# Attention, mixture of experts and FFN on one core: the third batch's loads of k and q move behind a store of x

## The chip, the core and the metric

The kernel runs on one core of a Trainium2 chip. The metric is device time in microseconds (us), and lower is better. The core has five instruction streams that matter here. TensorE (PE in the profile, PEld for its weight loads) multiplies and transposes. VectorE (DVE) and ScalarE (ACT) do element work. GpSimd (POOL) does small additions. SyncE (SP) computes nothing: in this kernel it asks for nearly all the direct transfers between memory and the core. Each stream runs its instructions in the order in which the program gives them.

## The reference

Three parts follow one another: block-causal attention over 4 batches of 8 heads (576 positions, head size 64), then a mixture of 8 experts with one expert for each token, then a dense FFN.

```python
scores = scale * np.matmul(q, k.transpose(0, 1, 3, 2))        # q, k, v: (4, 8, 576, 64)
scores = np.where(block_i >= block_j, scores, -1000000000.0)  # blocks of 64
attn = np.exp(scores - scores.max(-1, keepdims=True))
attn = attn / (attn.sum(-1, keepdims=True) + 1e-09)
x = np.matmul(attn, v).transpose(0, 2, 1, 3).reshape(2304, 512)
# expert e for the tokens whose gate is largest at e
out[mask] = gate_w[mask, None] * (np.maximum(xe @ w1[e], 0.0) @ w2[e])
# dense FFN
h = x @ w_in
g = np.maximum(h, 0.0) + np.log1p(np.exp(-np.abs(h)))
return g @ w_out
```

## The kernel before

Only the attention at the start (the first 240 us or so) matters for this change. It works on 16 **pairs** of heads, numbered 0 to 15. A batch has four pairs, so the first batch is pairs 0 to 3, the second 4 to 7 and the third 8 to 11. For a pair p the program transposes k and q (Kta.p, Qta.p, Ktb.p, Qtb.p, line 332), multiplies the scores (S0.p, S1.p, S2.p, line 378), takes maxima on DVE (line 384) and exponentials on ACT (line 389), transposes the probabilities (T, line 395), multiplies them with v (V.p, line 410), turns the result back into rows of x (Xa.p, Xb.p on PE, line 425) and scales these rows by the softmax's sums (xa.p, xb.p on DVE, lines 443 and 444). The scaled rows go into the tile xs, and xo.p stores them to the scratch tensor xd with two transfers asked for on SP (lines 450 and 451). Pairs overlap: while S0.p, S1.p and S2.p run, V.(p-1) follows and the rows of pair p-2 are made. What stands from one S0.p to the next is called **stage p** below.

The order of all this is written out by hand in one long string, SCHEDULE. Each word of it is one step, and the steps are issued in that order, each to its engine. Two buffers tie the steps together:

- xs exists once (line 436), so xa.p may not write it before both transfers of xo.(p-1) have landed.
- The tag ps2, a bank pair of PSUM, also exists once. The accumulators that xa.p and xb.p read (psx, line 421) and the widest scores of S0.(p+2) and S1.(p+2) (s4, line 356) share it. So S1.(p+2) may not start its part s4 before xb.p has read psx.

The loads of a batch b are the steps b1.0 to b1.17, b2.0 to b2.17 and so on (line 291): six transfers of k (four of 256 KB, two of 128 KB), then six of q, then six of v. They fill one of two buffers for each of k, q and v, so the third batch's k and q take the buffers of the first batch and wait on PE until Ktb.3 and Qtb.3 have read those. The first batch is loaded in slices of heads (f0 to f47, line 280). At the start of the kernel all these loads stand in one line on SP. The transfers asked for on SP use eight completion semaphores in turn (DMAHW0 to DMAHW7): a transfer waits on SP until the one eight places ahead of it has landed, and a step that needs a transfer's end waits for its semaphore.

```python
    XS[p][1] = work.tile([128, 5, 2, D], F32, tag="xs", name="xs", bufs=1)       # line 436, in x_out
    nc.sync.dma_start(xv[0:64], xs[0:64, 0]...)                                  # line 450, in x_st
    nc.sync.dma_start(xv[64:].rearrange("(c p) e -> p c e", p=128), xs[:, 1:5]...)
```

Of the kernel before, what the change touches and what calls it, by code (L numbers as in the profile page):

```python
# [20 lines left out]
NT, DM, E, F1, F2 = 2304, 512, 8, 1024, 2048  # L21
# [36 lines left out]
h21.0 h01.0 Klb.2 m30.1 S2.1 m41.1 e30.1 m20.1 T11.0 e41.1 m00.1 T30.0 m10.1 e00.1 m21.1 h11.0 m11.1 e20.1 h30.0 V.0  # L58
e10.1 e21.1 e11.1 Xr.1 F1.0 S0.2 F0.0 m40.2 T10.1 T20.1 m31.2 h10.1 Kta.3 e40.2 h20.1 T00.1 Qta.3 m01.2 Kha.3 T31.1
h00.1 Kla.3 Xa.0 Qha.3 h31.1 e31.2 Xb.0 Qla.3 T21.1 e01.2 xa.0 T01.1 xb.0 xo.0 b1.10 b1.11 f42 f43 f44 f45 f46 f47  # L60
b1.12 b1.13 b1.14 b1.15 b1.16 b1.17 Ktb.3 Qtb.3 h01.1 h21.1 S1.2 b2.0 La.0 b2.1 b2.2 b2.3 Qhb.3 b2.4 b2.5 Khb.3 b2.6
b2.7 Qlb.3 b2.8 b2.9 Klb.3 b2.10 b2.11 m30.2 S2.2 m41.2 e30.2 m20.2 T11.1 e41.2 m00.2 T30.1 m10.2 e00.2 m21.2 h11.1
m11.2 e20.2 h30.1 V.1 e10.2 e21.2 e11.2 Xr.2 F1.1 S0.3 F0.1 m40.3 T10.2 T20.2 m31.3 h10.2 Kta.4 e40.3 h20.2 T00.2 Qta.4
m01.3 Kha.4 T31.2 h00.2 Kla.4 Xa.1 Qha.4 h31.2 e31.3 Xb.1 Qla.4 T21.2 e01.3 xa.1 T01.2 xb.1 xo.1 Ktb.4 Qtb.4 h01.2
h21.2 S1.3 La.1 et Qhb.4 Khb.4 Qlb.4 Klb.4 m30.3 S2.3 m41.3 e30.3 m20.3 T11.2 e41.3 m00.3 T30.2 m10.3 e00.3 m21.3 h11.2
m11.3 e20.3 h30.2 V.2 e10.3 e21.3 e11.3 Xr.3 F1.2 S0.4 F0.2 m40.4 T10.3 T20.3 m31.4 h10.3 Kta.5 e40.4 h20.3 T00.3 Qta.5
m01.4 Kha.5 T31.3 h00.3 Kla.5 Xa.2 Qha.5 h31.3 e31.4 Xb.2 Qla.5 T21.3 e01.4 xa.2 T01.3 xb.2 xo.2 Ktb.5 Qtb.5 h01.3
h21.3 S1.4 La.2 Qhb.5 Khb.5 Qlb.5 Klb.5 m30.4 S2.4 m41.4 e30.4 m20.4 T11.3 e41.4 m00.4 T30.3 m10.4 e00.4 m21.4 h11.3
# [1523 lines left out]
```

## Time and profile before

| | |
|---|---|
| median of three runs | 903.48 us (903.44 to 903.62) |
| the profiled execution | 902.99 us |
| its span, first to last instruction | 901.3 us |
| PE busy | 876.0 us (97%) |
| DVE busy | 663.8 us (74%) |
| ACT busy | 562.9 us (62%) |
| mean granted TensorE clock | 0.995 of full speed |

The profiled execution took 902.99 us, 1.69 us more than its span, and the median of the runs is 0.49 us above it. All times inside the kernel are counted from the start of the span. A stretch of idle time of PE counts as time of the kernel where nothing else could have run; idle time of the other engines counts only where PE waits for them.

### The profile page before, as it was taken

The page shows a single profiled execution, that of the slowest core. Times are in us where ns is not written, and L with a number is a line of the kernel's source. Part 1 is how long each engine was busy: PE and PEld are TensorE (multiplying, and loading weights), DVE is VectorE, ACT ScalarE, POOL GpSimd, SP SyncE. Part 2 cuts the span into 40 slices and gives each one's busy share as a digit, 9 for nine tenths or more (in the row PEclk, how much of TensorE's full clock was granted, in tenths as well). Part 3 has the DMA queues.
Part 4 walks back from the last instruction along what each step waited for, and adds up shares of the span by engine and source line. Part 5 has one row for each costly group of instructions (what it writes and reads, how often), then busy time and mean ns, then how long its engine had stood idle before and what let it go on. Part 6 is the DMA issues. An engine that isn't in the chain of part 4 may idle for free.

```text
span 901.3 us, 17961 instructions
## 1 busy us (share of the span) xinstructions
PE 876.0 (97%) x6165; PEld 768.5 (85%) x6165; DVE 663.8 (74%) x1502; ACT 562.9 (62%) x1252; POOL 131.6 (15%) x165
## 2 busy tenths in 40 slices
PE   8979999999999999999999999999999999999997
PEld 5867887787899889999898887888788999999997
DVE  5656768968699898865764567676676569888975
ACT  5655676668556577655855688787778734343332
POOL 1010000010112252222310100000000001541421
PEclk9998999999999999999999999999999999999999
DMA  5894722433424468976361566466665883434323
GB/s 117 184 196 86 144 54 55 159 85 121 143 83 135 151 204 281 316 246 219 116 215 59 161 220 202 164 203 220 229 247 198 247 305 116 153 116 143 129 71 106
DMA packets 138486, 148.63 MB, mean 165 GB/s; under 512 B 70800, under 2 KB 95888, under 8 KB 138385
## 3 DMA queue, kind: packets, MB, share of 16 engines
q1 hardware_dynamic: 132240, 132.37, 48.5%
q0 software_dynamic: 4800, 14.70, 4.8%
q8 instruction: 50, 0.82, 0.4%
q10 hardware_dynamic: 1344, 0.33, 0.2%
q14 instruction: 52, 0.42, 0.2%
HBM read 119.56 MB, written 41.43 MB: 179 GB/s over the span
## 4 chain that ended last, share of the span: by engine, by line
PE 56%; DVE 4%; DMA 3%; issue 1%; ACT 1%; SPq 1%; DVEq 0%; ACTq 0%
PE yps L1062 3%; PE yps L1063 3%; PE yps L1064 3%; PE fh L1206 3%; PE fh L1207 3%; PE fh L1205 3%; PE hps L1027 3%; PE hps L1028 3%; PE hps L1029 3%; DMA gq<-gd 2%; PE fX L1206 2%; PE fX L1207 2%; PE fX L1205 2%; PE fY L1206 2%; PE fY L1207 2%; PE fY L1205 2%
## 5 line engine op out<-in xcount | busy, mean ns | idle before, releaser
L1335 ACT CAST ah<-sum 128x1280 fp32r<-128x1280 f32 (+1 forms) x40 | 46.3, 1157 | 107.6 <-DVE sum L1328 40.5
L389 ACT ACTIVATE P<-s,negm 128x448 f32<-128x448 f32 (+4 forms) x160 | 82.7, 528 | 32.8 <-DVE negm L384 32.8
L1027 PE MATMUL hps<-xh,H1h 128*128 128x256 f32 x320 | 90.8, 284 | 0.2 <-DVE hl L1047 0.2
L1029 PE MATMUL hps<-xh,H1l 128*128 128x256 f32 x320 | 90.5, 283 | 0.0
L1028 PE MATMUL hps<-xl,H1h 128*128 128x256 f32 x320 | 90.5, 283 | 0.0
L384 DVE TENSOR_REDUCE negm<-s 128x1 f32<-128x576 f32 (+4 forms) x160 | 68.3, 479 | 19.1 <-PE s L378 19.0
L983 DVE TENSOR_TENSOR H2l<-R,H2h 128x512 fp32r<-128x512 f32 x96 | 63.6, 687 | 25.4 <-ACT H2h L979 22.2
L1400 POOL DMA_INDIRECT out_dram<-fos,OI x16 | 47.2, 2952 | 198.8 <-DVE fos L1392 154.8
L979 ACT CAST H2h<-R 128x512 fp32r<-128x512 f32 x96 | 57.5, 624 | 27.2 <-PE yps L1063 11.9
L395 PE MATMUL pt<-ident,P 128*128 128x128 f32 x480 | 68.8, 280 | 3.0 <-DVE PT L400 2.0
L1062 PE MATMUL yps<-H2h,hh 128*128 128x512 f32 x176 | 71.6, 407 | 0.2 <-PEq L1532 0.2
L378 PE MATMUL s<-kZ,qZ 64*128 64x288 f32 (+4 forms) x576 | 62.0, 328 | 9.9 <-DVE lg L444 7.1
L1063 PE MATMUL yps<-H2h,hl 128*128 128x512 f32 x176 | 68.8, 391 | 0.0
L1064 PE MATMUL yps<-H2l,hh 128*128 128x512 f32 x176 | 68.7, 390 | 0.0
L983 DVE TENSOR_TENSOR H1l<-R,H1h 128x512 fp32r<-128x512 f32 x96 | 62.3, 685 | 8.3 <-ACT H1h L979 6.3
L378 PEld LDWEIGHTS s<-kZ,qZ 64*128 64x128 f32 x576 | 52.6, 193 | 18.4 <-issue 13.4
L979 ACT CAST H1h<-R 128x512 fp32r<-128x512 f32 x96 | 55.5, 622 | 16.2 <-PE hps L1028 11.5
L1339 DVE TENSOR_TENSOR al<-sum,ah 128x1280 fp32r<-128x1280 f32 (+1 forms) x40 | 54.2, 1356 | 13.5 <-ACT ah L1335 13.5
L1027 PEld LDWEIGHTS hps<-xh,H1h 128*128 128x128 f32 x320 | 61.3, 192 | 0.8 <-DVE hl L1047 0.4
L1028 PEld LDWEIGHTS hps<-xl,H1h 128*128 128x128 f32 x320 | 61.3, 192 | 0.3
L1029 PEld LDWEIGHTS hps<-xh,H1l 128*128 128x128 f32 x320 | 61.3, 192 | 0.0
L395 PEld LDWEIGHTS pt<-ident,P 128*128 128x128 f32 x480 | 53.1, 142 | 7.0 <-DVE PT L400 2.7
(361 smaller groups left out, 2623.6 us busy)
## 6 DMA issues: line engine op xcount, KB each, us to landing
R<-in_moe_w_dram SPq DMA_DIRECT2D x96, 512.0 KB
gd<-ft SPq DMA_DIRECT2D x64, 256.0 KB
gq<-gd SPq DMA_DIRECT2D x64, 256.0 KB
dbw<-in_moe_w_out_dram SPq DMA_DIRECT2D x32, 256.0 KB
dbl<-in_moe_w_in_dram SPq DMA_DIRECT2D x22, 256.0 KB
yg<-yd SPq DMA_DIRECT2D x4, 1026.0 KB
xd<-xs SPq DMA_DIRECT2D x16, 256.0 KB
wd<-ah SPq DMA_DIRECT2D x4, 896.0 KB
```

The source lines that it names most:

```text
L378: mm(o, lhsT=a, rhs=b, start=first, stop=last)
L384: nc.vector.tensor_reduce(m[0:n], SC[p, j, c][0:n], axis=AX.X, op=ALU.max, negate=True)
L389: nc.scalar.activation(t[0:n, 0:NK[c]], SC.pop((p, j, c))[0:n], AF.Exp, bias=NM.pop((p, j, c))[0:n], scale=1.0, accum_out=rs[p % 4][0:n, c ...
L395: nc.tensor.transpose(ps[:, o:o + 128], P[p, j, c][:, 128 * kc:128 * kc + 128], ident)
L979: nc.scalar.copy(HW[l, i][0], raw(l, i))
L983: TT(l_, raw(l, i), h.bitcast(F32), op=ALU.subtract)
L1027: mm(a, lhsT=wh, rhs=xh, start=(k == 0), stop=False)
L1028: mm(a, lhsT=wh, rhs=xl, start=False, stop=False)
L1029: mm(a, lhsT=wl, rhs=xh, start=False, stop=(k == 3))
L1062: mm(o, lhsT=h[:, c], rhs=wh, start=(f == 0), stop=False)
L1063: mm(o, lhsT=l[:, c], rhs=wh, start=False, stop=False)
L1064: mm(o, lhsT=h[:, c], rhs=wl, start=False, stop=(f == 7))
```

## The change

The twelve steps b2.0 to b2.11 (the third batch's k and q) leave their place around S1.2 and stand around S1.3, one stage later in SCHEDULE, behind xo.1. No step is added or removed, and no other step changes its place. The six loads of the third batch's v (b2.12 to b2.17) stay where they were.

```diff
-b1.12 b1.13 b1.14 b1.15 b1.16 b1.17 Ktb.3 Qtb.3 h01.1 h21.1 S1.2 b2.0 La.0 b2.1 b2.2 b2.3 Qhb.3 b2.4 b2.5 Khb.3 b2.6
+b1.12 b1.13 b1.14 b1.15 b1.16 b1.17 Ktb.3 Qtb.3 h01.1 h21.1 S1.2 La.0 Qhb.3 Khb.3 Qlb.3 Klb.3 m30.2 S2.2 m41.2 e30.2
...
-h21.2 S1.3 La.1 et Qhb.4 Khb.4 Qlb.4 Klb.4 m30.3 S2.3 m41.3 e30.3 m20.3 T11.2 e41.3 m00.3 T30.2 m10.3 e00.3 m21.3 h11.2
+T21.2 e01.3 xa.1 T01.2 xb.1 xo.1 Ktb.4 Qtb.4 h01.2 h21.2 S1.3 b2.0 La.1 b2.1 b2.2 b2.3 et Qhb.4 b2.4 b2.5 Khb.4 b2.6
```

Of all engines only SP has its instructions in another order. On SP, from the second batch's v (vraw_145) to the store of pair 2's rows (xs_1105), the kernel before has this; kraw_146 and qraw_147 are the third batch's k and q, and xs_869 holds pair 1's rows:

```order
L291 DMA vraw_145<-in_v_dram 128x8x64 x4
L291 DMA vraw_145<-in_v_dram 64x8x64 x2
L291 DMA kraw_146<-in_k_dram 128x8x64 x4
L291 DMA kraw_146<-in_k_dram 64x8x64 x2
L291 DMA qraw_147<-in_q_dram 128x8x64 x4
L291 DMA qraw_147<-in_q_dram 64x8x64 x2
L450 DMA xd_97<-xs_869 64x128
L451 DMA xd_97<-xs_869 128x4x128
L450 DMA xd_97<-xs_1105 64x128
L451 DMA xd_97<-xs_1105 128x4x128
```

The changed kernel has this in the same place on SP; pair 1's rows are called xs_857 there:

```order
L291 DMA vraw_145<-in_v_dram 128x8x64 x4
L291 DMA vraw_145<-in_v_dram 64x8x64 x2
L450 DMA xd_97<-xs_857 64x128
L451 DMA xd_97<-xs_857 128x4x128
L291 DMA kraw_146<-in_k_dram 128x8x64 x4
L291 DMA kraw_146<-in_k_dram 64x8x64 x2
L291 DMA qraw_147<-in_q_dram 128x8x64 x4
L291 DMA qraw_147<-in_q_dram 64x8x64 x2
L450 DMA xd_97<-xs_1105 64x128
L451 DMA xd_97<-xs_1105 128x4x128
```

The store of pair 1's rows moves up past twelve loads; from the store of pair 2's rows on the row is the same again.

On DVE the steps keep their order. Around xa.2, which writes pair 2's rows into xs, the kernel before has these, with what each waits for in brackets:

```order
L349 SCALAR_TENSOR_TENSOR kZ_1078<-psT_1058,kZ_1078 128x512 [waits Activation_49]
L400 COPY PT3_1093<-pt_1080 128x320 [waits PE_49]
L349 SCALAR_TENSOR_TENSOR qZ_1091<-psT_1071,qZ_1091 128x512 [waits Activation_49]
L443 TENSOR_TENSOR xs_1105<-psx_1087,rinv_784 128x384 [waits DMAHW1_49,DMAHW0_49,PE_49]
L444 TENSOR_TENSOR lg_787<-psx_1087,rinv_784 128x48 [waits Pool_49]
```

And the changed kernel has these in the same place on DVE:

```order
L349 SCALAR_TENSOR_TENSOR kZ_1078<-psT_1058,kZ_1078 128x512 [waits Activation_49]
L400 COPY PT3_1093<-pt_1080 128x320 [waits PE_49]
L349 SCALAR_TENSOR_TENSOR qZ_1091<-psT_1071,qZ_1091 128x512 [waits Activation_49]
L443 TENSOR_TENSOR xs_1105<-psx_1087,rinv_772 128x384 [waits DMAHW5_49,DMAHW4_49,PE_49]
L444 TENSOR_TENSOR lg_775<-psx_1087,rinv_772 128x48 [waits Pool_49]
```

Both wait for the two transfers of xo.1; only the semaphores that these carry are others, since they stand twelve places earlier on SP.

## Rows read from the trace of the kernel before

**Rows 1.** The page: busy time, and three lines of the 40 slices.

```profile
span 901.3 us, 17961 instructions
PE 876.0 (97%) x6165; PEld 768.5 (85%) x6165; DVE 663.8 (74%) x1502; ACT 562.9 (62%) x1252; POOL 131.6 (15%) x165
...
PE   8979999999999999999999999999999999999997
...
PEclk9998999999999999999999999999999999999999
DMA  5894722433424468976361566466665883434323
```

**Rows 2.** Waits of PE, whole span: engine, line, releaser: total us, times, longest.

```profile
PE s L378 <- DVE lg L444: 7.1, 1, 7.1
PE fY L1368 <- DVE al L1339: 2.1, 3, 1.1
PE pt L395 <- DVE PT L400: 2.0, 3, 0.9
```

**Rows 3.** Timeline of PE: start, length, line, operation, count, idle before.

```profile
28.89 0.92 PE L378 MATMUL s<-kZ,qZ 64*128 64x288 f32 x8
...
41.97 0.92 PE L378 MATMUL s<-kZ,qZ 64*128 64x288 f32 x8
...
55.26 0.93 PE L378 MATMUL s<-kZ,qZ 64*128 64x288 f32 x8
...
61.49 0.47 PE L378 MATMUL s<-kZ,qZ 64*128 64x448 f32 x1
69.04 1.29 PE L378 MATMUL s<-kZ,qZ 64*128 64x288 f32 x6 [7.08 <-DVE lg L444]
...
77.42 0.92 PE L378 MATMUL s<-kZ,qZ 64*128 64x288 f32 x8
...
90.55 0.92 PE L378 MATMUL s<-kZ,qZ 64*128 64x288 f32 x8
...
103.71 0.93 PE L378 MATMUL s<-kZ,qZ 64*128 64x288 f32 x8
...
105.84 0.60 PE L332 MATMUL psT<-ident,kraw 128*128 128x128 f32 x4
```

**Rows 4.** Timeline of DVE around xb.1 and xa.2.

```profile
48.26 0.18 DVE L444 TENSOR_TENSOR lg<-psx,rinv 128x32 f32<-128x32 f32 x1
...
60.02 0.68 DVE L349 SCALAR_TENSOR_TENSOR qZ<-psT,qZ 128x512 fp32r<-128x512 f32 x1
67.80 0.56 DVE L443 TENSOR_TENSOR xs<-psx,rinv 128x384 f32<-128x384 f32 x1 [7.09 <-DMA xd<-xs]
```

**Rows 5.** Timeline of SP: each row is transfers being asked for.

```profile
39.13 0.53 SPq L451 DMA_DIRECT2D xd<-xs  x1
...
44.04 0.61 SPq L280 DMA_DIRECT2D vraw<-in_v_dram  x1
...
44.70 6.09 SPq L291 DMA_DIRECT2D vraw<-in_v_dram  x6
50.89 6.26 SPq L291 DMA_DIRECT2D kraw<-in_k_dram  x6
57.66 6.12 SPq L291 DMA_DIRECT2D qraw<-in_q_dram  x6
63.88 0.58 SPq L450 DMA_DIRECT2D xd<-xs  x1
64.55 0.53 SPq L451 DMA_DIRECT2D xd<-xs  x1
```

**Rows 6.** Windows: stretch, busy time by engine, granted PE clock, DMA share, GB/s.

```profile
51.00:54.00 3.00, 3.00 (x20) 1.67 (x20) 1.97 (x7) 3.00 (x13) 0.89 (x3) 1.00 0.97 189
...
64.00:66.00 2.00, 0.00 (x0) 0.00 (x0) 0.00 (x0) 0.00 (x0) 0.00 (x0) 1.00 0.91 190
66.00:67.00 1.00, 0.00 (x0) 0.00 (x0) 0.00 (x0) 0.00 (x0) 0.00 (x0) 1.00 0.66 187
67.00:73.50 6.50, 4.46 (x33) 4.22 (x34) 3.97 (x12) 1.57 (x5) 0.54 (x2) 0.50 0.17 46
...
74.00:77.00 3.00, 3.00 (x22) 1.29 (x22) 1.13 (x5) 2.32 (x9) 0.00 (x0) 1.00 0.00 0
```

More of the change, by code (lines that the diff above doesn't have):

```diff
@@ L60 @@
 h00.1 Kla.3 Xa.0 Qha.3 h31.1 e31.2 Xb.0 Qla.3 T21.1 e01.2 xa.0 T01.1 xb.0 xo.0 b1.10 b1.11 f42 f43 f44 f45 f46 f47
-b1.12 b1.13 b1.14 b1.15 b1.16 b1.17 Ktb.3 Qtb.3 h01.1 h21.1 S1.2 b2.0 La.0 b2.1 b2.2 b2.3 Qhb.3 b2.4 b2.5 Khb.3 b2.6
-b2.7 Qlb.3 b2.8 b2.9 Klb.3 b2.10 b2.11 m30.2 S2.2 m41.2 e30.2 m20.2 T11.1 e41.2 m00.2 T30.1 m10.2 e00.2 m21.2 h11.1
-m11.2 e20.2 h30.1 V.1 e10.2 e21.2 e11.2 Xr.2 F1.1 S0.3 F0.1 m40.3 T10.2 T20.2 m31.3 h10.2 Kta.4 e40.3 h20.2 T00.2 Qta.4
-m01.3 Kha.4 T31.2 h00.2 Kla.4 Xa.1 Qha.4 h31.2 e31.3 Xb.1 Qla.4 T21.2 e01.3 xa.1 T01.2 xb.1 xo.1 Ktb.4 Qtb.4 h01.2
-h21.2 S1.3 La.1 et Qhb.4 Khb.4 Qlb.4 Klb.4 m30.3 S2.3 m41.3 e30.3 m20.3 T11.2 e41.3 m00.3 T30.2 m10.3 e00.3 m21.3 h11.2
+b1.12 b1.13 b1.14 b1.15 b1.16 b1.17 Ktb.3 Qtb.3 h01.1 h21.1 S1.2 La.0 Qhb.3 Khb.3 Qlb.3 Klb.3 m30.2 S2.2 m41.2 e30.2
+m20.2 T11.1 e41.2 m00.2 T30.1 m10.2 e00.2 m21.2 h11.1 m11.2 e20.2 h30.1 V.1 e10.2 e21.2 e11.2 Xr.2 F1.1 S0.3 F0.1 m40.3
+T10.2 T20.2 m31.3 h10.2 Kta.4 e40.3 h20.2 T00.2 Qta.4 m01.3 Kha.4 T31.2 h00.2 Kla.4 Xa.1 Qha.4 h31.2 e31.3 Xb.1 Qla.4
+T21.2 e01.3 xa.1 T01.2 xb.1 xo.1 Ktb.4 Qtb.4 h01.2 h21.2 S1.3 b2.0 La.1 b2.1 b2.2 b2.3 et Qhb.4 b2.4 b2.5 Khb.4 b2.6
+b2.7 Qlb.4 b2.8 b2.9 Klb.4 b2.10 b2.11 m30.3 S2.3 m41.3 e30.3 m20.3 T11.2 e41.3 m00.3 T30.2 m10.3 e00.3 m21.3 h11.2
 m11.3 e20.3 h30.2 V.2 e10.3 e21.3 e11.3 Xr.3 F1.2 S0.4 F0.2 m40.4 T10.3 T20.3 m31.4 h10.3 Kta.5 e40.4 h20.3 T00.3 Qta.5
```

## The prediction

> **What bounds the kernel now.** I read the page first. PE is busy for 97% of the span, and its line of slices holds 9s almost throughout [rows 1]. So the kernel is bound by PE, and a change is worth what it gives back of PE's idle time, or of time in which PE runs at a low clock. The line of the granted clock shows one dip, in the fourth slice (about 68 to 90 us). The reader is to see that this one place is out of the ordinary. The waits of PE name it: the longest by far is a single one of 7.1 us, at the scores of line 378, ended by the instruction of line 444 on DVE; the next group holds 2.1 us in three waits [rows 2].
>
> The timeline of PE shows where it stands. S1.4 issues one matmul at 61.49 us and the next at 69.04 us [rows 3]. That second one writes s4, which shares PSUM with psx, so it waits for xb.2 on DVE. DVE is idle for 7.09 us before xa.2 and starts it at 67.80 us; what ended the idle time is a transfer from xs to xd [rows 4], the store of pair 1's rows. The timeline of SP then tells why that store was late: pair 1's rows were ready at 48.44 us (48.26 + 0.18, [rows 4]), but SP asks for twelve loads of the third batch's k and q from 50.89 us on, and only then, at 63.88 us, for the store [rows 5]. The chain is SP's line, then the store's landing, then xa.2 and xb.2, then PE. Nothing computes in the gap.
>
> **What the place costs.** A stage is counted from one S0 to the next. The S0 of stages 2 to 7 start at 28.89, 41.97, 55.26, 77.42, 90.55 and 103.71 us [rows 3], so the stages last 13.08, 13.29, **22.16**, 13.13 and 13.16 us. The mean of the four that have no stall is 52.66 / 4 = 13.17 us, so stage 4 is 22.16 - 13.17 = 8.99 us too long. Measured against the longest neighbour the excess is 8.87 us, against the shortest 9.08 us. Of it 7.08 us are the wait itself. The other 1.9 us is slow work: PE is granted a clock of 0.50, the lower of its two levels (1.2 GHz), from 67.00 to 73.50 us, after standing idle, and 1.00 again in the stretch from 74.00 us [rows 6].
>
> The Trainium skill (TensorE: Matmul & The Clock Gate, Terms) puts the penalty of a throttled stretch at its length times one less the share of the clock. By that estimate, the 4.46 us that PE is busy in the slow stretch [rows 6] would cost 2.23 us, stage 4 would be 9.3 us too long, and the time would come out 0.3 us lower than the sum below. The stage lengths say 1.9 us and are what I use, since they also hold whatever of the slow work was not bound by PE's clock.
>
> **The change part by part.** Nothing is added or removed. The two transfers of xo.1 move ahead of twelve loads on SP; every other engine keeps its order.
>
> *The store.* SP has asked for the second batch's v by 50.79 us (44.70 + 6.09, [rows 5]), and the rows have been ready since 48.44 us. So SP asks for xo.1 at 50.9 us, 13 us earlier than now, and is done at about 52.1 us, as the two took from 63.88 to 65.08 us [rows 5]. How long it takes to land is bounded by two rows. From below: now it is asked for by 65.08 us and xa.2 starts at 67.80 us, 2.7 us later, with loads in front of it too. From above: pair 0's store was asked for by 39.66 us, and the sixth transfer of the row of v loads, eight places behind it, could be asked for at 44.04 us only because that store had landed [rows 5], so it took at most 4.4 us in the midst of the loads. So xo.1 lands between 54.8 and 56.5 us. DVE wants to start xa.2 at 60.70 us (60.02 + 0.68, [rows 4]). The store is there 4 us earlier by the worse bound, and the wait of 7.09 us is gone. I take 2.7 us, the row of the same store; between the bounds nothing changes in the sum.
>
> *The loads that are moved.* All twelve, and the queue behind them on SP, move by the store's 1.2 us. They now run from 50.89 to 63.78 us (57.66 + 6.12, [rows 5]) and will end at about 65.0 us. Their data is first read by the transposes of pair 8 at 105.84 us [rows 3], which come at 96.8 us once 9.0 us are gone. They have more than 25 us to spare, so this costs nothing. They wait for PE's transposes of pair 3, which lie in stage 2 and so are over by 41.97 us [rows 3]; that wait has long ended when SP reaches it.
>
> *What is late next.* Behind the twelve loads stands the store of pair 2's rows, xo.2. Its rows will be ready at about 61.7 us, but SP gets to it at 65.0 us. It is asked for by 66.2 us and lands at 68.9 us, or at 70.6 us by the upper bound. xa.3 wants xs one stage after xa.2, at 60.70 + 13.17 = 73.87 us. So 3.3 to 5.0 us remain, and no new wait appears. Behind xo.2 SP's order is unchanged, and its next loads wait for PE, not for the clock on the wall.
>
> *The clock.* With no gap PE has nothing to cool down on, so the slow stretch goes with the wait.
>
> **Sum.** The profiled execution took 902.99 us (span 901.3 and 1.69 around it). Less 9.0 us that is 894.0 us. The median of the runs stands 0.49 us higher, at 903.48 us, so the forecast for the median is **894.5 us**. The later parts run as before, only earlier: PE's other waits are for DVE and ACT [rows 2], and these move with it. Their lengths may change as transfers fall differently, and I allow half of the 2.1 us of the largest such group as a gain and all of it as a loss. That gives 893.4 to 896.6 us.
>
> **The rivals.**
>
> *A store still waits for loads.* The store cannot pass loads that were asked for before it, and the transfer engines are 91% to 97% busy here [rows 6]. The Trainium skill (DMA: Bandwidth & Descriptors, Queues, rings and completion order) says that the increment of a completion semaphore lands only after every earlier write from that transfer engine, which would bind xo.1 to the v loads in front of it and xo.2 to the k and q loads; no row here shows one engine's writes. The price is worked out from the rows: it decides where a store lags by more than 8.6 us (xo.1, from 52.1 to 60.70) or 7.7 us (xo.2, from 66.2 to 73.87). Against it stand the lags of 2.7 us and at most 4.4 us above. If half of the old wait stayed, 3.5 us, with half of the slow clock, 1.0 us, the time would be 894.5 + 4.5 = 899.0 us. Chance 0.04.
>
> *No change.* The wait goes, but the time is given back where the kernel waits for transfers further on, or the wait moves whole to xa.3 (7.1 + 1.9 us again). For it: the DMA line reaches 8 and 9 in later slices [rows 1]. Against it: PE's slices are 9 there all the same, and the two largest groups of PE's waits behind the one that goes hold 2.1 and 2.0 us and are ended by DVE [rows 2]. That gives 903.5 us. Chance 0.03.
>
> *Slower: the third batch comes too late.* The loads are asked for later, and pair 8's transposes at 96.8 us wait for them. This starts to cost where the last load lands after 96.8 us, and the kernel is slower than before by over 0.2% from a landing at 96.8 + 9.0 + 1.8 = 107.6 us on; at 110 us it would be about 905.9 us. The rows put the last load at about 65 us asked for and speak for a landing a few us later, as the DMA share falls to 0.17 behind 67 us, two or three us after the last load was asked for [rows 5, 6]. Chance 0.02.
>
> That the change doesn't do what it says is ruled out by the order of SP, in which the store stands ahead of the loads.
>
> **How the numbers follow.** Forecast 0.91, a remaining or moved wait 0.04, no change 0.03, slower 0.02. The range of the forecast, 893.4 to 896.6 us, holds most of the 0.91 and leaves out the rivals, so it stands as the range for 8 in 10. A measurement of this kernel can tell about 0.2%, 1.8 us, from no change. The forecast and the remaining wait are both faster by more than that: 0.95. Within 0.2%: 0.03. Slower: 0.02.
>
> **What would show each step.** In the timeline of SP the store of pair 1 starts near 50.9 us and the loads of k near 52.1 us. In that of DVE xa.2 starts near 60.7 us with no wait for a transfer, and xa.3 near 73.9 us. In that of PE the S0 of stage 5 starts near 68.4 us instead of 77.42, the wait of 7.1 us is missing from the waits, and the granted clock is 1.00 from 67 to 74 us. The pair 8 transposes start near 96.8 us. The prediction is wrong if xa.2 or xa.3 still shows a wait for the transfer from xs to xd, or if the attention ends 9 us earlier and the end of the kernel does not.

## The result

The changed kernel took 895.28 us (median of four runs, 894.40 to 895.94) against 903.46 us for the kernel before on the same chip (901.69 to 903.62). The ratio is 0.9913, with a 95% interval of 0.9896 to 0.9930. A second set of runs, `after_again` below, gave 893.52 us (891.74 to 894.64) against 903.12 us, a ratio of 0.9889 (0.9870 to 0.9908). The forecast was 894.5 us in a range of 893.4 to 896.6 us, and both medians lie in it. The ratios, here and below, are not quotients of the two medians, and differ from these by up to 0.0012. The profiled execution took 894.68 us where that of before took 902.99 us, 8.31 us less.

The waits of PE over the whole span (engine, line, releaser: total us, times, longest) no longer hold the single wait that led [rows 2]:

```profile
PE pt L395 <- DVE PT L400: 2.0, 3, 0.9
PE warm L498 <- DVE mrow L305: 1.4, 1, 1.4
PE s L378 <- DVE kZ L349: 1.3, 2, 1.0
PE fY L1368 <- DVE al L1339: 1.2, 3, 0.6
```

The timeline of SP in the changed kernel answers to [rows 5]. The store of pair 1's rows stands ahead of the loads of k and q, and that of pair 2's rows behind them:

```profile
51.06 0.58 SPq L450 DMA_DIRECT2D xd<-xs  x1
51.73 0.53 SPq L451 DMA_DIRECT2D xd<-xs  x1
52.39 5.56 SPq L291 DMA_DIRECT2D kraw<-in_k_dram  x6
58.05 6.77 SPq L291 DMA_DIRECT2D qraw<-in_q_dram  x6
64.92 0.58 SPq L450 DMA_DIRECT2D xd<-xs  x1
65.59 0.53 SPq L451 DMA_DIRECT2D xd<-xs  x1
```

The timeline of DVE, for [rows 4], shows the first write of xa.2 and of xa.3. Neither has a bracket, so neither waited:

```profile
60.69 0.55 DVE L443 TENSOR_TENSOR xs<-psx,rinv 128x384 f32<-128x384 f32 x1
...
73.83 0.55 DVE L443 TENSOR_TENSOR xs<-psx,rinv 128x384 f32<-128x384 f32 x1
```

The timeline of PE, for [rows 3], has the S0 of stages 4 to 7 and the first transposes of pair 8:

```profile
55.30 0.92 PE L378 MATMUL s<-kZ,qZ 64*128 64x288 f32 x8
...
68.45 0.92 PE L378 MATMUL s<-kZ,qZ 64*128 64x288 f32 x8
...
81.59 0.93 PE L378 MATMUL s<-kZ,qZ 64*128 64x288 f32 x8
...
94.73 0.93 PE L378 MATMUL s<-kZ,qZ 64*128 64x288 f32 x8
...
96.85 0.60 PE L332 MATMUL psT<-ident,kraw 128*128 128x128 f32 x4
```

Stage 4 lasts 68.45 - 55.30 = 13.15 us instead of 22.16, as long as its neighbours (13.14 us each). Stage 7 starts 8.98 us earlier than before (103.71 - 94.73). The stretch that had been slow [rows 6] is now full of work at the full clock (stretch, then busy time of PE, PEld, DVE, ACT, POOL, granted clock, DMA share, GB/s):

```profile
67.00:73.50 6.50, 6.50 (x64) 6.04 (x61) 3.90 (x10) 4.51 (x12) 0.00 (x0) 1.00 0.79 164
```

**Where 0.67 us of the 8.98 went.** The lead is the time by which an instruction starts earlier than in the kernel before. By the first transpose of the FFN (line 1181) it had shrunk to 483.2 - 475.5 = 7.7 us. In between, the profile of the changed kernel has a slow stretch that the profile of before has not. Its second profile, from `after_again`, has none at that place either. First the two windows of the first profile, then those of the second:

```profile
171.00:174.00 3.00, 2.27 (x27) 1.63 (x29) 2.03 (x8) 1.78 (x8) 0.00 (x0) 0.88 0.02 5
174.00:177.00 3.00, 3.00 (x12) 0.98 (x10) 1.18 (x9) 1.81 (x8) 0.00 (x0) 0.55 0.82 203
```

```profile
171.00:174.00 3.00, 2.30 (x29) 1.72 (x31) 2.03 (x8) 1.80 (x7) 0.00 (x0) 1.00 0.02 5
174.00:177.00 3.00, 3.00 (x29) 1.82 (x26) 1.38 (x10) 2.31 (x9) 0.00 (x0) 1.00 0.80 191
```

PE had the same idle time in 171 to 174 us in both (0.73 and 0.70 us), and yet the clock fell in one. The stretch lies in stage 12, which starts at 160.97 us in both. The starts of stages 12 and 13 in the first profile, of stage 13 in the second, and of both in the kernel before:

```profile
160.97 0.92 PE L378 MATMUL s<-kZ,qZ 64*128 64x288 f32 x8
...
178.13 0.92 PE L378 MATMUL s<-kZ,qZ 64*128 64x288 f32 x8
```

```profile
176.41 0.93 PE L378 MATMUL s<-kZ,qZ 64*128 64x288 f32 x8
```

```profile
169.88 0.93 PE L378 MATMUL s<-kZ,qZ 64*128 64x288 f32 x8
...
185.35 0.92 PE L378 MATMUL s<-kZ,qZ 64*128 64x288 f32 x8
```

Stage 12 lasts 178.13 - 160.97 = 17.16 us in the first profile, 176.41 - 160.97 = 15.44 us in the second and 185.35 - 169.88 = 15.47 us in the kernel before. So that slow stretch cost 1.7 us in the first profile, and the change did not bring it about every time. In the second profile the lead at the FFN's first transpose is 483.2 - 474.0 = 9.2 us. The rest of the difference arises later: from that transpose to the last scaled rows of the output the kernel before took 414.1 us, the changed one 413.5 us in the first profile and 414.9 us in the second.

### The profile page after: what moved, and what is told of

It reads as the page before. It is cut to its first block, busy times and chain, and to the rows that moved or that the text cites. A ratio compares the mean times of both kernels' runs of the same rounds, so it can differ in the third digit from the quotient of the medians.

```text
span 893.0 us, 17960 instructions
## 1 busy us (share of the span) xinstructions
PE 876.1 (98%) x6165; PEld 768.1 (86%) x6165; DVE 663.7 (74%) x1502; ACT 563.1 (63%) x1252; POOL 131.7 (15%) x165
## 4 chain that ended last, share of the span: by engine, by line
PE 57%; DMA 4%; DVE 3%; SPq 1%; issue 1%; ACT 1%; DVEq 0%
PE yps L1062 3%; PE yps L1064 3%; PE yps L1063 3%; DMA gq<-gd 3%; PE hps L1028 3%; PE hps L1029 3%; PE hps L1027 3%; PE fh L1206 3%; PE fh L1207 3%; PE fh L1205 3%; PE fX L1206 2%; PE fX L1207 2%; PE fY L1206 2%; PE fY L1207 2%; PE fX L1205 2%; PE fY L1205 2%
## 5 line engine op out<-in xcount | busy, mean ns | idle before, releaser
L410 PE MATMUL o<-PT,vraw 128*64 128x512 f32 (+4 forms) x384 | 58.6, 439 | 0.0
```

## The experiments

Each kernel ran beside the kernel before on the same chip. The theory under test (A) is the prediction's: xa.2 waits for xs until the store of pair 1's rows has landed, and the place of that store in SP's line is all that the change alters.

**The wait taken away without moving a load.** In the kernel before, pair 1's rows get a tile of their own, R1_0, which is still unused at that time; a second line of the edit, not shown, hands it to this function.

```diff
-            XS[p][1] = work.tile([128, 5, 2, D], F32, tag="xs", name="xs", bufs=1)
+            XS[p][1] = pools["R1"][:, 0:640].rearrange("p (c h d) -> p c h d", c=5, h=2) if p == 1 else work.tile([128, 5, 2, D], F32, tag="xs", name="xs", bufs=1)
```

> The kernel before, with its order untouched (the store of pair 1's rows stays behind the twelve loads), but pair 1's rows of x go into a tile of their own (the still unused R1_0), so that xa.2 does not have to wait for that store. Theory A (the stall is xa.2 waiting for xs to come free, and the store's place on SP matters through that alone): the store is still asked for at about 63.9 us, xa.2 starts at 60.7 us with no wait, stage 4 lasts 13.2 us, the time is 894.5 to 895.5 us, the same as the changed kernel. Rival B (the gain of the change comes from the loads themselves running later, away from other traffic or other work): the loads run as before, so the time stays at 903.5 us or moves by less than 2 us.

Measured: 893.31 us against 903.13 us, ratio 0.9885 (0.9868 to 0.9901). The timeline of SP has the store as late as ever, and that of DVE has xa.2 without a wait (its execution already runs about 0.5 us behind that of the changed kernel at the start of stage 3):

```profile
63.34 0.58 SPq L450 DMA_DIRECT2D xd<-R  x1
64.02 0.53 SPq L451 DMA_DIRECT2D xd<-R  x1
```

```profile
61.15 0.55 DVE L443 TENSOR_TENSOR xs<-psx,rinv 128x384 f32<-128x384 f32 x1
```

The order of the loads does not matter where nothing waits for the store. Theory A stands and rival B falls.

**Both together.** The changed kernel with the same tile of its own.

> The change and the tile of its own for pair 1's rows together. Theory A: both take away the same wait, so together they give what each gives alone, 893 to 895.5 us (ratio 0.989 to 0.991). If they gave different things, the gains would add: below 890 us.

Measured: 893.64 us (891.94 to 897.42), ratio 0.9884 (0.9865 to 0.9903). The gains do not add. The slowest of its four executions is the profiled one, which again has a slow stretch at 174 to 177 us, at a clock of 0.54.

**Half of the loads, and ten of twelve, ahead of the store.** b2.0 to b2.5 (then b2.0 to b2.9) keep the place of before, and the rest leave it and stand behind S1.3. The diff shows the place behind S1.3 in the first of the two; long lines of SCHEDULE are cut at their ends, here and below.

```diff
-h21.2 S1.3 La.1 et Qhb.4
+h21.2 S1.3 b2.6 b2.7 b2.8 b2.9 b2.10 b2.11 La.1 et Qhb.4
```

> Half of the change: the six loads of the third batch's k stay ahead of the store of pair 1's rows, the six of q go behind it. Theory A (xa.2 starts when the store has landed, 2.7 us after SP has asked for it, or at 60.7 us, whichever is later): the store is asked for from 57.2 to 58.4 us, lands at 61.1 us, xa.2 waits 0.4 us, the clock stays at 1.00, the time is 895.0 to 896.0 us. Rival C (the store lands only when the whole batch of loads has been moved, since the transfers share the engines): landing near 67 us wherever the store stands in the queue, xa.2 waits about 7 us, 903.5 us; half of the loads moved gives half of the gain: 899 us.

> Ten of the twelve loads stay ahead of the store of pair 1's rows (all of k, four of q), the last two of q go behind it. Theory A: the store is asked for from 62.0 to 63.2 us, lands at 65.9 us, xa.2 waits 5.2 us. Stage 4 lasts 13.2 + 5.2 us, and up to 1.9 us more if PE's clock falls in that gap: 899.7 us with the clock at 1.00, 901.6 us with a slow stretch as long as before. Rival C (the wait is set by the end of the loads' data): 7.1 us and 903.5 us as before, since the same data is in flight.

Measured: 895.57 us (893.38 to 898.27) for half, ratio 0.9904 (0.9884 to 0.9925), and 901.72 us for ten, ratio 0.9982 (0.9970 to 0.9994). The profile of the kernel with half, SP, DVE and PE in turn:

```profile
58.31 0.52 SPq L451 DMA_DIRECT2D xd<-xs  x1
```

```profile
62.53 0.56 DVE L443 TENSOR_TENSOR xs<-psx,rinv 128x384 f32<-128x384 f32 x1 [1.76 <-DMA xd<-xs]
```

```profile
55.30 0.93 PE L378 MATMUL s<-kZ,qZ 64*128 64x288 f32 x8
63.77 0.78 PE L378 MATMUL s<-kZ,qZ 64*128 64x288 f32 x6 [1.76 <-DVE lg L444]
73.16 0.92 PE L378 MATMUL s<-kZ,qZ 64*128 64x288 f32 x8
```

And that of the kernel with ten, SP, DVE and PE in turn:

```profile
62.49 0.53 SPq L451 DMA_DIRECT2D xd<-xs  x1
```

```profile
65.68 0.56 DVE L443 TENSOR_TENSOR xs<-psx,rinv 128x384 f32<-128x384 f32 x1 [4.84 <-DMA xd<-xs]
```

```profile
55.38 0.93 PE L378 MATMUL s<-kZ,qZ 64*128 64x288 f32 x8
...
76.11 0.93 PE L378 MATMUL s<-kZ,qZ 64*128 64x288 f32 x8
```

The wait follows the store's place and ends 2.7 us (65.68 - 63.02) to 3.7 us (62.53 - 58.83) after SP has asked for it, as A says. Rival C's reading in these two runs, that the end of the loads' data sets it, falls: half of the loads moved gave well over half of the gain. What A missed is the price of a short wait. The waits were put at 0.4 and 5.2 us and came to 1.8 and 4.8 us. But stage 4 lasts 73.16 - 55.30 = 17.86 us with half, 4.7 us too long, so 2.9 us of it are not the wait. The windows of the kernel with half show slow work:

```profile
64.00:71.00 7.00, 7.00 (x42) 4.78 (x42) 4.19 (x13) 4.32 (x15) 0.27 (x1) 0.53 0.72 138
```

Behind a gap of 1.76 us the clock fell in this execution, and the slow work cost more than the gap.

> Half of the change once more (k ahead of the store, q behind). In its first profile xa.2 waited 1.8 us and PE's clock fell behind that gap: stage 4 lasted 17.9 us, 2.9 us of it slow clock; the four executions split into two at a mean clock of 1.00 (893.4 and 894.7 us) and two below (896.5 and 898.3 us). Theory D (whether the clock falls behind so short a gap differs from one execution to the next, and costs 2.5 to 3.5 us when it does): again two groups, apart by that much and ordered by their mean clock, median between 894 and 897 us. If the gap alone decides: all executions like the first profile, 896.5 to 898.5 us, or all near 895 us.

Measured: 896.14 us (894.17 to 896.82), ratio 0.9913 (0.9897 to 0.9928). This profile has a wait of 1.29 us and no slow stretch behind it:

```profile
61.91 0.56 DVE L443 TENSOR_TENSOR xs<-psx,rinv 128x384 f32<-128x384 f32 x1 [1.29 <-DMA xd<-xs]
```

```profile
64.00:71.00 7.00, 7.00 (x67) 5.21 (x65) 3.85 (x12) 4.66 (x16) 0.00 (x0) 1.00 0.64 119
```

All six executions of this set have a mean clock of 0.999 or 1.00, and their times do not fall into two groups. So the clock fell behind a gap of 1.8 us once for certain and did not behind one of 1.3 us. Theory D's two groups did not show again, and how often such a short gap costs the clock stays open.

**The gap filled.** The kernel before, with 33 matmuls whose result nothing reads, ahead of S1.4.

```diff
-h21.3 S1.4 La.2
+h21.3 u9 S1.4 La.2
...
-    calls.update({f"u{i}": lambda n=n: warm(n) for i, n in enumerate((8, 2, 3, 2, 1, 2))})
+    calls.update({f"u{i}": lambda n=n: warm(n) for i, n in ((0, 8), (1, 2), (2, 3), (3, 2), (4, 1), (5, 2), (9, 33))})
```

> The kernel before with 33 matmuls of 512 columns, whose result nothing reads, put on PE just ahead of S1.4, so that PE works through the gap of 7.1 us; the order of SP is untouched. It separates the two parts of the excess of stage 4. Theory A (7.1 us of wait and 1.9 us of slow clock behind it): xa.2 still waits until 67.8 us, the granted clock stays at 1.00 from 67 to 74 us, stage 4 lasts 20.2 to 20.8 us instead of 22.2, the time is 901.5 to 902.3 us. If the 1.9 us is not the clock but work that piled up on DVE and ACT during the gap: no gain, 903.5 us.

Measured: 902.09 us (900.41 to 903.55), ratio 0.9985 (0.9975 to 0.9994). xa.2 waits 6.70 us, the granted clock is 1.00 throughout stage 4, and the stage lasts 75.44 - 55.35 = 20.09 us in place of 22.16:

```profile
55.35 0.93 PE L378 MATMUL s<-kZ,qZ 64*128 64x288 f32 x8
...
75.44 0.93 PE L378 MATMUL s<-kZ,qZ 64*128 64x288 f32 x8
```

```profile
67.00:73.50 6.50, 6.50 (x53) 4.20 (x52) 5.10 (x15) 2.77 (x10) 0.54 (x2) 1.00 0.17 45
```

2.07 us are gained, of which 0.39 us is the shorter wait, so the slow clock cost about 1.7 us behind the full gap. The median shows half of it, 1.0 us, and its interval starts at 0.5 us. The profiled execution, the slowest, had a slow stretch elsewhere (714 to 720 us, behind a wait of 2.92 us at line 1367).

**The next store pushed back.** The changed kernel, with the six loads of q asked for twice, so that pair 2's store stands behind 18 loads.

```diff
-        return [lambda o=o, i=i: nc.sync.dma_start(o, i) for o, i in l]
+        return [lambda m=[n] + ([6, 7, 8, 9, 10, 11] if (b, n) == (2, 11) else []): [nc.sync.dma_start(*l[j]) for j in m] for n in range(18)]
```

> The changed kernel, with the six loads of the third batch's q asked for a second time, right behind the first, so that the store of pair 2's rows stands behind 18 loads instead of 12. It measures the margin that the next store has. Theory A (xa.3 starts at 73.8 us or when that store has landed, 2.7 us after SP has asked for it): the store is asked for from about 71.5 to 72.7 us, lands at 75.4 us, xa.3 waits 1.6 us, nothing else changes: 896.5 to 897.5 us. If loads ahead of a store cost in proportion to their number wherever they stand: 6/12 of 9.0 us, 899.5 us.

Measured: 894.57 us (893.72 to 896.20), ratio 0.9906 (0.9882 to 0.9930), between the two medians of the changed kernel. The store was asked for by 71.65 us, and xa.3 waited a quarter of a microsecond; the view names PE as what ended that wait:

```profile
57.07 13.28 SPq L291 DMA_DIRECT2D qraw<-in_q_dram  x12
70.39 0.63 SPq L450 DMA_DIRECT2D xd<-xs  x1
71.06 0.59 SPq L451 DMA_DIRECT2D xd<-xs  x1
```

```profile
74.59 0.56 DVE L443 TENSOR_TENSOR xs<-psx,rinv 128x384 f32<-128x384 f32 x1 [0.26 <-PE pt L395]
```

The expected 1.6 us is missed, since SP was done with the loads 1.1 us earlier than I had reckoned. A store asked for 5.5 us later than in the changed kernel (71.65 against 66.12) costs 0.4 us at most (stage 5 lasts 82.38 - 68.85 = 13.53 us against 13.14), so the margin that the prediction gave the next store, 3.3 to 5.0 us, was there, and a cost in proportion to the number of loads falls.

**The loads pushed back further.** The changed kernel with the twelve loads behind the store of pair 3's rows (at S1.5), then behind that of pair 4's (at S1.6); the diff shows the first of the two.

```diff
-h21.2 S1.3 b2.0 La.1 b2.1 b2.2 b2.3 et Qhb.4 b2.4 b2.5 Khb.4 b2.6
+h21.2 S1.3 La.1 et Qhb.4 Khb.4
...
-h21.4 S1.5 La.3
+h21.4 S1.5 b2.0 b2.1 b2.2 b2.3 b2.4 b2.5 b2.6 b2.7 b2.8 b2.9 b2.10 b2.11 La.3
```

> The changed kernel with the third batch's loads of k and q moved two stages further, behind the store of pair 3's rows. Theory A (the loads only have to land before pair 8's transposes at 96.9 us): they are asked for from about 75.8 to 88.5 us, land at about 91 us, and nothing waits: 894.4 to 896 us as the changed kernel. The rival that was put on the slower side (a later third batch costs) gives more than that.

> The same loads moved one stage further still, behind the store of pair 4's rows. Theory A: k is asked for from about 88.7 to 94.5 us and lands by about 97 us, q from 94.5 to 101 us; pair 8's transposes of q at 97.8 us wait for q's first four loads until about 101 us, and those of the rest until 103.5 us, so PE stands still for 3 to 4 us in stage 7: 898 to 900 us, up to 901 us if the clock falls. It shows at what point the slower rival would have decided. If the loads' landing does not gate these transposes: 895 us.

Measured: 893.21 us (892.61 to 893.54), ratio 0.9890 (0.9868 to 0.9912), two stages later, and 900.29 us (898.62 to 901.90), ratio 0.9971 (0.9957 to 0.9984), three stages later. The first is the changed kernel again. In the second, PE waits for the loads at pair 8's transposes:

```profile
94.61 0.93 PE L378 MATMUL s<-kZ,qZ 64*128 64x288 f32 x8
99.11 0.30 PE L332 MATMUL psT<-ident,qraw 128*128 128x128 f32 x1 [1.26 <-DVE kZ L349]
100.23 0.47 PE L332 MATMUL psT<-ident,qraw 128*128 128x128 f32 x1 [0.82 <-DMA qraw<-in_q_dram]
...
114.45 0.92 PE L378 MATMUL s<-kZ,qZ 64*128 64x288 f32 x8
```

Stage 7 lasts 19.84 us, 6.7 us too long. Three waits ended by the loads come to 2.5 us. The view puts the wait of 1.26 us ahead of them down to DVE, but in the changed kernel the same transposes start at 97.80 us, before that step of DVE has started, so it is more likely a load too. The rest goes with a granted clock of 0.50 to 0.51 from 100 to 106 us, which the expectation had allowed for. The rival that the prediction put on the slower side exists, then, but the loads begin to cost only where they are asked for at some time between 75.6 us (two stages later) and 88.6 us (three).

**The loads on another queue.** The kernel before, with the twelve loads asked for by POOL.

```diff
-        return [lambda o=o, i=i: nc.sync.dma_start(o, i) for o, i in l]
+        return [lambda o=o, i=i, e=(nc.gpsimd if b == 2 and n < 12 else nc.sync): e.dma_start(o, i) for n, (o, i) in enumerate(l)]
```

> The kernel before, with the third batch's loads of k and q asked for by POOL in the place where they stand in the program, so that SP's line holds only the store behind the second batch's v, while the same bytes move at the same time. Theory A (SP's line makes the store late, not the traffic): the store is asked for when SP has done the second batch's v, xa.2 does not wait or waits under 1 us: 893.5 to 896 us, unless the loads on POOL, which then start at about 35 us beside the first batch's last slices of v and the second batch's v, make SP's own loads slower. Rival C (the transfers are what limits, SP only keeps pace with them): SP's loads of v take longer by what POOL's loads move in that time, the store is asked for several us later than 50.9 us and xa.2 still waits: 897 to 904 us.

Measured: 904.63 us (899.57 to 908.78), ratio 1.0012 (0.9994 to 1.0031): no gain, and theory A's number fails, in the way that its reservation allowed for. SP's six loads of the first batch's v took 15.17 us to be asked for, in place of 3.58 us, and so the store was asked for only at 61.46 us. PE stood still one stage earlier, for the second batch's q: stage 3 lasts 65.02 - 42.31 = 22.71 us. When xa.2 came, at 70.39 us, it did not wait. First SP in the kernel before, then SP, PE and DVE in this one:

```profile
41.07 3.58 SPq L280 DMA_DIRECT2D vraw<-in_v_dram  x6
```

```profile
40.88 15.17 SPq L280 DMA_DIRECT2D vraw<-in_v_dram  x6
...
61.46 0.58 SPq L450 DMA_DIRECT2D xd<-xs  x1
```

```profile
55.64 0.45 PE L332 MATMUL psT<-ident,qraw 128*128 128x128 f32 x1 [7.11 <-DMA qraw<-in_q_dram]
```

```profile
70.39 0.55 DVE L443 TENSOR_TENSOR xs<-psx,rinv 128x384 f32<-128x384 f32 x1
```

The windows from 36 to 51 us, before and in this run, show how little a second queue added: the last figure, in GB/s, is 206 before and 232 here:

```profile
36.00:51.00 15.00, 14.89 (x144) 12.48 (x141) 11.06 (x33) 9.69 (x31) 2.27 (x15) 1.00 0.95 206
```

```profile
36.00:51.00 15.00, 12.53 (x116) 10.41 (x114) 10.08 (x30) 9.04 (x29) 11.92 (x27) 1.00 1.12 232
```

So rival C of this run is borne out in the main, though not in what it said of xa.2: in this stretch the transfers are the limit with either queue, and a load that is not yet needed takes its time from whatever stands beside or behind it. SP's line was the order in which this limited resource was handed out. This run had the loads start some 15 us earlier than before, at 35.7 us, so it doesn't tell what another queue would do at the same moment.

## Why the prediction was right

- *The place and the chain.* Right, and shown: with the store as late as before but a tile of its own behind it, the whole gain appears (`e1_own_tile`).
- *The size.* Put at 9.0 us, between 8.87 and 9.08; measured 8.98 us at the start of stage 7. Its two parts were put at 7.1 us of wait and 1.9 us of slow clock. Filling the gap gave back about 1.7 us of the second. The estimate from the Trainium skill (TensorE: Matmul & The Clock Gate, Terms), 2.23 us, was the larger of the two and further off.
- *The store's landing.* Put at 2.7 us and at most 4.4 us after SP has asked for it; measured 2.5 to 3.7 us where xa.2 waited for it (`e4_warm`, `e3_ten_ahead`, `e2_k_ahead`). In the changed kernel it was asked for by 52.26 us and not waited for at 60.69 us.
- *The next store and the moved loads.* Right in both margins: 5.5 us more before the next store cost 0.4 us at most, and two stages more for the loads cost nothing that can be measured. The price of the slower rival was added up wrongly: by its own condition a landing at 110 us is 13.2 us late, which gives 894.5 + 13.2 = 907.7 us and not 905.9. The forecast does not use it.
- *The rest of the kernel.* An allowance of 1 us below and 2 us above was needed: the first profile gave back 0.67 us on balance, and a slow stretch in it, which comes and goes from execution to execution, cost 1.7 us. The two medians of the same kernel lie 0.8 us above and 1.0 us below the forecast, so that a single median came this close is in part luck; the 8.98 us at stage 7 is not.
- *What was too simple.* The rival of a remaining wait was priced with half the wait and half the slow clock, in proportion. The runs show no proportion: a wait of 1.8 us brought 2.9 us of slow clock, one of 4.8 us brought 2.7 us (20.73 us of stage 4, less 13.15 and 4.84), the full one of 7.1 us about 1.9 us. And I read SP's line as the limit, where the transfers set its pace (`e8_pool_queue`); for this change the two give the same sum.

## What to carry to other kernels

Where a queue of transfers is saturated, its order is a priority list: put what something waits for soon (here a store that frees a single buffer) ahead of loads that are needed 45 us later. Measure a stall by the length of the stage that holds it against its neighbours, since the slow clock behind it is in that length and not in the table of waits. Before moving a load back, look up the first instruction that reads it: here two more stages were free, and the third cost 6.7 us.

## What the runs showed of the hardware

A gap of 1.76 us on PE was followed by a granted clock of 0.53 over 7 us in one execution, and one of 1.29 us by none in another. In stage 12 the clock fell to 0.54 to 0.56 for a 3 us window in three profiles (the changed kernel, `e5_q_twice`, `e7_after_own_tile`), and it stayed at 1.00 there in the other ten, those of `after_again` and the kernel before among them. Stage 12 lasted 17.14 to 17.16 us in the three and 15.44 to 15.47 us in the ten, whichever kernel it was. The idle time of PE ahead of it does not tell them apart: from 171 to 174 us it is 0.98 us in `e5_q_twice` and in `e1_own_tile`, and only the first fell. What decides it is open.

> The changed kernel once more, with another profile. Of the 9.0 us that stage 4 gave back in its first profile, 1.8 us were missing by about 185 us, behind a stretch from 172 to 178 us at a granted clock of 0.5 to 0.8, which the kernel before did not have in its profile. If this slow stretch is a matter of the single execution (PE's waits ahead of it were the same in both): it is gone or somewhere else in this profile, and the shift against the kernel before is about 9.0 us behind that place too. If the change causes it: it is there again at 172 to 178 us. Time 894.4 to 896.0 us.

That run's place is the one told with the result: the slow stretch was gone, and the lead was 9.2 us behind it.
